# Attention and bilinear kernel: k's stack apart, each load behind its buffer's last use, four weighing visits, and a first unit on VectorE with more filler matmuls

## The chip, the core and the metric

The kernel runs on one core of one Trainium2 chip. The metric is the device time of one execution in microseconds (us). TensorE (PE) multiplies matrices; its weight loads are listed apart as PEld. VectorE is DVE, ScalarE is ACT, GpSimd is POOL, and SyncE (SP) issues the DMAs. TensorE writes to PSUM, which has eight banks; everything else lives in SBUF.

## The reference

```python
q_rot, k_rot = rotate(q), rotate(k)              # 4 batches, 8 heads, 576 positions, 64 wide
attn = softmax(q_rot @ k_rot.T / 8)
x = (attn @ v)                                   # as 2304 tokens x 512
h = elu(x @ w_in) @ w_out                        # 512 -> 2048 -> 512
out = ((h @ w1) * (h @ w2)) @ w3 @ w_out2        # 512 -> 1024 -> 512
```

All in float32. `rotate` multiplies by tables of cosines and sines and adds the two halves.

## The kernel before

The attention is a list of 16 **units** (a batch and a pair of heads). A unit has nine **steps**: four chunks of 128 queries times two heads, and one step for the last 64 queries of both heads. In step n of the loop at line 496 TensorE makes the scores `s` of the step two ahead (L286; L278 for the last step of a unit and for the whole first unit), then what the table `todo` holds for step n, then the four transposes `ptp` of the probabilities of step n (L334). VectorE takes the row maximum (`nm`, L298), ScalarE the exponential (`pr`, L302). The transposes are copied out of PSUM in the next step by ScalarE or VectorE (L316, L318). All this is written in a fixed order per engine (`manual_schedule`), and each engine works its list in order.

The values are weighed in **visits**: `weigh` multiplies the transposed probabilities with v into a PSUM tile `o` (L392, 64-column products, two halves of a unit's queries; L394 and L397 for the last 64 keys, tile `plT`), and one step after the last visit of a half VectorE multiplies by the reciprocal sums into `xT` (L406). Six visits of L392 and two of L394 fall on a unit.

The next unit's q and k are rotated meanwhile: on POOL two products (`turn`, L184), a sum (`add`, L187), then ScalarE copies the high part of the float32r split (`high`, L80), and POOL subtracts for the low part (`low`, L193). `stack` then moves the parts by DMA into tile `st` (L260, L263), from which the scores read. POOL also spreads the reciprocals (`rb`, L84), fills `diag` (L84), and does the last step of one weight tile in each of twelve units (L125), each time in the first step of units 2 to 13. ROPE and STACK give the steps of these pieces, NORM, SPREAD, NTURN and PV those of the weighing.

The first unit is rotated in pieces before the loop (`first_rope`), shared by VectorE and POOL. `warm_up` issues matmuls of a tile of zeros, which write nothing that is used. After the attention come the two feed-forward parts, whose text is the same in both kernels.

Of the kernel before, what the change touches and what calls it, by code (L numbers as in the profile page):

```python
# [18 lines left out]
P = 128  # L19
# [38 lines left out]
def kernel(  # L58
# [81 lines left out]
    with ExitStack() as c1:  # L140
# [94 lines left out]
        def first_rope(u):  # L235
            for w, at_, to, eng, steps in (
                (1, 0, 352, dve, (0, 1, 2)), (0, 0, 256, dve, (0, 1, 2)),
                (1, 0, 352, dve, (3, 4)), (0, 0, 256, dve, (3, 4)),
                (1, KD, SK, pool, (0, 1, 2)), (1, 352, KD, dve, (0, 1, 2)), (1, 352, SK, dve, (3, 4)),
                (0, 256, S, pool, (0, 1, 2)),  # L240
            ):
# [9 lines left out]

        def stack(u):

            st = stacks[u] = st_p.tile([P, 2, 3, S], F32R, tag="st", name="st")
            for j in range(2):
                c = (SK, S)[j]
                for e in range(2):
                    part = hls[u][64 * j:64 * j + 64, e].bitcast(F32)
                    both = part[:, :2 * c].rearrange("p (w c) -> p w c", w=2)[:, :, :S]
                    nc.sync.dma_start(st[64 * e:64 * e + 64, j, 0:2].bitcast(F32), both)  # L260
                for e in range(2):
                    part = hls[u][64 * j:64 * j + 64, 1 - e].bitcast(F32)
                    nc.sync.dma_start(st[64 * e:64 * e + 64, j, 2].bitcast(F32), part[:, c:c + S])  # L263

# [56 lines left out]
        def turn(g):  # L321
# [60 lines left out]

        def weigh(n, u, hf, kc):
            nq = HALF[hf][1]
            if kc == 0:
# [4 lines left out]
            if kc < 4:  # L390
                for j in range(2):
                    pe.matmul(o[64 * j:64 * j + 64], vj[:, j, kc], th[:, j, kc], start=(kc == 0), stop=False)  # L392
                return
            pe.matmul(o[:, :256], vs[u][:, 2 * NKC * D:], tl[:, :256], start=False, stop=not hf)  # L394
            if hf:
                for j in range(2):
                    pe.matmul(  # L397
                        o[64 * j:64 * j + 64, 256:], vj[:64, j, 4], tl[:64, 256 + 64 * j:320 + 64 * j],
                        start=False, stop=True,
                    )  # L400
            at(n + 1, weighed, u, hf)

# [29 lines left out]
        for i, u in enumerate(units):  # L432
            n = 9 * i
            if i + 2 < len(units):
                at(n + LOAD_QK, load, units[i + 2], 1)
                at(n + LOAD_QK, load, units[i + 2], 0)
            if i + 1 < len(units):
                v_ = units[i + 1]
                at(n + LOAD_V, load_v, v_)
                if i == 0:  # L440
                    steps = part(u, 0, 256, S, dve, act, dve)
                    for k_ in (3, 4):
                        at(FIRST[0][k_ - 3], steps[k_])
                    at(FIRST[0][2], diagonal, u)
# [34 lines left out]
        with tc.manual_schedule():  # L479
# [277 lines left out]
```

## Time and profile before

| | |
|---|---|
| device time, median of 3 runs | 1051.91 us (1050.37 to 1052.35) |
| the profiled execution | 1052.59 us, span 1050.8 us |
| TensorE busy | 1037.8 us, 99% of the span |
| POOL busy between 40 and 250 us | 0.82 to 0.90 of the time |
| granted TensorE clock, mean | 0.986 |

The span is what the trace covers; the profiled execution's own time is 1.8 us longer. A busy TensorE is not one at its peak: ends of matmuls are modelled. The attention takes the first 305 us, the rest is matmuls of 512 columns.

### The profile page before, as it was taken

The page shows a single profiled execution, that of the slowest core. Times are in us where ns is not written, and L with a number is a line of the kernel's source. Part 1 is how long each engine was busy: PE and PEld are TensorE (multiplying, and loading weights), DVE is VectorE, ACT ScalarE, POOL GpSimd, SP SyncE. Part 2 cuts the span into 40 slices and gives each one's busy share as a digit, 9 for nine tenths or more (in the row PEclk, how much of TensorE's full clock was granted, in tenths as well). Part 3 has the DMA queues.
Part 4 walks back from the last instruction along what each step waited for, and adds up shares of the span by engine and source line. Part 5 has one row for each costly group of instructions (what it writes and reads, how often), then busy time and mean ns, then how long its engine had stood idle before and what let it go on. Part 6 is the DMA issues. An engine that isn't in the chain of part 4 may idle for free.

```text
span 1050.8 us, 14641 instructions
## 1 busy us (share of the span) xinstructions
PE 1037.8 (99%) x5590; PEld 865.4 (82%) x5590; DVE 568.3 (54%) x978; ACT 463.7 (44%) x921; POOL 257.9 (25%) x260
## 2 busy tenths in 40 slices
PE   8999999999999999999999999999999999999998
PEld 7767767777777888888888999989888888889997
DVE  4678878778767996668667653212313214122321
ACT  2567666667546756556545644322211212112121
POOL 4698889888510010001000000000100000000000
PEclk7799999999999999999999999999999999999999
DMA  4687878786756015545555523536400101001000
GB/s 157 190 233 213 232 221 216 211 236 198 172 211 242 1 40 180 180 160 180 181 180 180 181 101 127 193 120 220 143 0 1 41 1 41 1 1 41 1 31 31
DMA packets 46390, 138.84 MB, mean 132 GB/s; under 512 B 5488, under 2 KB 7152, under 8 KB 46320
## 3 DMA queue, kind: packets, MB, share of 16 engines
q1 hardware_dynamic: 46320, 137.91, 41.6%
q8 instruction: 44, 0.72, 0.3%
q14 instruction: 26, 0.21, 0.1%
HBM read 85.66 MB, written 25.69 MB: 106 GB/s over the span
## 4 chain that ended last, share of the span: by engine, by line
PE 90%; SPq 3%; DMA 3%; DVE 1%; POOL 1%; issue 1%; ACTq 0%; ACT 0%; DVEq 0%
PE h L537 19%; PE y L564 19%; PE a L537 9%; PE b L537 9%; PE y L674 9%; PE ptp L334 6%; PE o L392 5%; PE s L286 5%; PE w L615 4%; DMA st<-hl 3%; PE s L278 2%; SPq L263 2%; SPq L260 1%; PE o L394 1%; POOL hl L193 1%
## 5 line engine op out<-in xcount | busy, mean ns | idle before, releaser
L537 PE MATMUL h<-xt,w 128*128 128x512 f32 (+1 forms) x960 | 213.4, 368 | 0.0
L564 PE MATMUL y<-g,w 128*128 128x512 f32 (+1 forms) x960 | 212.5, 367 | 0.0
L537 PEld LDWEIGHTS h<-xt,w 128*128 128x128 f32 x960 | 175.2, 188 | 23.4 <-DVE e L552 0.2
L564 PEld LDWEIGHTS y<-g,w 128*128 128x128 f32 x960 | 175.2, 188 | 22.5
L76 POOL TENSOR_TENSOR xt<-xT,xt 128x512 fp32r<-128x512 f32 (+1 forms) x20 | 26.5, 1326 | 668.9 <-DVE xt L82 668.1
L302 ACT ACTIVATE pr<-s,nm 128x576 f32<-128x576 f32 x144 | 107.0, 743 | 100.8 <-DVE nm L298 99.9
L661 DVE TENSOR_TENSOR a<-b,a 128x512 f32<-128x512 f32 (+1 forms) x40 | 25.5, 637 | 180.0 <-PE b L537 180.0
L298 DVE TENSOR_REDUCE nm<-s 128x1 f32<-128x576 f32 x144 | 108.6, 754 | 25.7 <-PE s L286 11.7
L537 PE MATMUL a<-xt,w 128*128 128x512 f32 (+1 forms) x480 | 107.4, 368 | 0.0
L537 PE MATMUL b<-xt,w 128*128 128x512 f32 (+1 forms) x480 | 106.8, 367 | 0.0
L674 PE MATMUL y<-W,g 128*128 128x512 f32 x432 | 104.9, 390 | 0.0
L334 PEld LDWEIGHTS ptp<-idt,pr 128*128 128x128 f32 x576 | 63.4, 144 | 46.2 <-issue 23.7
L286 PE MATMUL s<-st 128*128 128x288 f32 x480 | 94.9, 316 | 4.4 <-DMA st<-hl 4.3
L537 PEld LDWEIGHTS a<-xt,w 128*128 128x128 f32 x480 | 88.2, 188 | 12.5
L537 PEld LDWEIGHTS b<-xt,w 128*128 128x128 f32 x480 | 87.7, 188 | 11.3
L334 PE MATMUL ptp<-idt,pr 128*128 128x128 f32 x576 | 96.4, 291 | 0.0
L674 PEld LDWEIGHTS y<-W,g 128*128 128x128 f32 x432 | 80.9, 188 | 16.1
L659 ACT ACTIVATE a<-a 128x512 f32<-128x512 f32 (+1 forms) x40 | 22.3, 556 | 139.2 <-PE a L537 139.2
L552 DVE SCALAR_TENSOR_TENSOR e<-e,h 128x512 f32<-128x512 f32 (+1 forms) x80 | 50.3, 631 | 61.1 <-ACT e L550 60.7
L184 POOL TENSOR_TENSOR raw_qk<-raw_qk,tab 128x640 f32<-128x640 f32 (+1 forms) x56 | 82.5, 1483 | 2.3
L549 ACT ACTIVATE e<-h 128x512 f32<-128x512 f32 (+1 forms) x80 | 44.2, 554 | 72.6 <-PE h L537 70.2
L286 PEld LDWEIGHTS s<-st 128*128 128x128 f32 x480 | 67.9, 189 | 7.0 <-issue 3.8
(301 smaller groups left out, 1275.0 us busy)
## 6 DMA issues: line engine op xcount, KB each, us to landing
kept<-w SPq DMA_DIRECT2D x40, 512.0 KB, 2.6
w<-kept SPq DMA_DIRECT2D x40, 512.0 KB, 3.3
st<-hl SPq DMA_DIRECT2D x60, 288.0 KB, 4.5
raw<-w_ SPq DMA_DIRECT2D x32, 512.0 KB, 3.6
raw_qk<-k_ SPq DMA_DIRECT2D x15, 640.0 KB, 6.1
raw_qk<-q_ SPq DMA_DIRECT2D x15, 576.0 KB, 5.1
st<-hl SPq DMA_DIRECT2D x60, 144.0 KB, 4.2
raw<-w_in_ SPq DMA_DIRECT2D x16, 512.0 KB, 5.1
```

The lines of the kernel that those rows point to most:

```text
L184: pool.tensor_tensor(r[:, z], r[:, z], tab[:, w, z, TAB[w]], op=ALU.mult)
L286: pe.matmul(s[:, n, :288], st[:, j, 0, c * P:c * P + P], st[:, j, z, n * 288:(n + 1) * 288], start=(z == 1), stop=(z == 2),)
L298: dve.tensor_reduce(nm, s[:, :, :288], axis=AX.XY, op=ALU.max, negate=True)
L302: act.activation(pr_t[u, c][:, j].rearrange("p (n i) -> p n i", n=2), s[:, :, :288], ACTF.Exp, bias=nm, accum_out=sums_t[u, hf][:, at_:at_ ...
L334: pe.transpose(pt[:, kc], pr[:, at_:at_ + P], idt)
L392: pe.matmul(o[64 * j:64 * j + 64], vj[:, j, kc], th[:, j, kc], start=(kc == 0), stop=False)
L537: pe.matmul(ps[:, :n], w[:, a, cc * P:(cc + 1) * P], x[cc][:, c], start=(i == 0), stop=(i == 11))
L549: act.activation(e, ps[:, :n], ACTF.Relu, scale=-1.0)
L552: dve.scalar_tensor_tensor(g, e, -1.0, ps[:, :n], op0=ALU.add, op1=ALU.max)
L564: pe.matmul(ys[ti][o][:, :n], wout[f][:, a, o * P:(o + 1) * P], g[:, c], start=(f == 0 and i == 0), stop=(f == NF - 1 and i == 2),)
L615: pe.matmul(ps, w3_t[i, j // 4][:, a, j % 4 * P:j % 4 * P + P], wo[j][:, c], start=(j == 0 and n == 0), stop=(j == 7 and n == 2),)
L674: pe.matmul(outs[ti][o], g[:, a, o * P:(o + 1) * P], wW[f][:, c], start=(f == 0 and i == 0), stop=(f == NG - 1 and i == 2),)
```

## The change

1. `stack(u, w)` runs for k and q apart, each right behind its own `low`; twelve DMAs of 144 KB take the place of four of 288 and four of 144 KB. q's `low` moves from step 4 to 3, k's from step 2 to -2.
2. A load of q or k is issued behind the `low` that frees its buffer, instead of both at step 4.
3. `weigh` takes several key chunks at once: four visits in place of six, with the L394 and L397 products inside them (the 64-key product now over 128 rows, below zeros).
4. PSUM: `ps_o` has one bank instead of two, `ps_t` three instead of two.
5. The first unit's rotation is on VectorE alone; POOL starts with the second unit's k. 30 filler matmuls at the start instead of 27, 4 more inside the first score, and 34 in the first eleven steps instead of 8.

```diff
-NTURN = (5, 11)
+NTURN = (6, 11)
 PV = (
-    (5, 0, (0,)), (6, 0, (1,)), (7, 0, (2, 3)), (8, 0, (4,)),
-    (10, 1, (0,)), (11, 1, (1,)), (12, 1, (2, 3)), (13, 1, (4,)),
+    (5, 0, (0, 1)), (7, 0, (4, 2, 3)), (10, 1, (0, 1)), (12, 1, (4, 2, 3)),
 )
-ROPE = ((-1, 0, 1, 1, 4), (-5, -4, -3, -3, 2))
-STACK = 4
+ROPE = ((-1, 0, 1, 1, 3), (-5, -4, -3, -3, -2))
+DIAG = 5
-WARM = 27
-FILL = (4, 2, 2)
+WARM = 30
+FILL = (4, 3, 4, 4, 4, 3, 3, 3, 2, 2, 2)
+FILL_IN = 4
...
-        ps_o = c1.enter_context(tc.tile_pool(name="ps_o", bufs=2, space=PSUM, reuse_waits="tile"))
-        ps_t = c1.enter_context(tc.tile_pool(name="ps_t", bufs=2, space=PSUM, reuse_waits="tile"))
+        ps_o = c1.enter_context(tc.tile_pool(name="ps_o", bufs=1, space=PSUM, reuse_waits="tile"))
+        ps_t = c1.enter_context(tc.tile_pool(name="ps_t", bufs=3, space=PSUM, reuse_waits="tile"))
...
             def low():
                 pool.tensor_tensor(lo, r[:, 0], hi.bitcast(F32), op=ALU.subtract)
-                if w == 0:
-                    diagonal(u)
+                stack(u, w)
+                m = units.index(u) + 2 - w
+                if m < len(units):
+                    load(units[m], 1 - w)
...
-                (1, KD, SK, pool, (0, 1, 2)), (1, 352, KD, dve, (0, 1, 2)), (1, 352, SK, dve, (3, 4)),
-                (0, 256, S, pool, (0, 1, 2)),
+                (1, 0, 352, dve, (3, 4)), (0, 0, 256, dve, (3, 4)), (1, 352, SK, dve, (0, 1, 2, 3, 4)),
```

Where POOL's list changes: one unit's worth in the middle of the attention. `raw_qk` 640 wide is k, 576 wide is q. Before:

```order
L84 TENSOR_SCALAR rb<-ri 128x256
L193 TENSOR_TENSOR hl<-raw_qk,hl 128x576
L84 TENSOR_SCALAR diag_108<-hl 64x2x64 x2
L184 TENSOR_TENSOR raw_qk<-raw_qk,tab 128x640 x2
L187 TENSOR_TENSOR raw_qk<-raw_qk 128x640
L184 TENSOR_TENSOR raw_qk<-raw_qk,tab 128x576
L125 TENSOR_TENSOR w<-wr,w 128x512
L84 TENSOR_SCALAR rb_113<-ri 128x256
L84 TENSOR_SCALAR rb_113<-ri 64x64 x2
...
L187 TENSOR_TENSOR raw_qk<-raw_qk 128x576
L193 TENSOR_TENSOR hl<-raw_qk,hl 128x640
```

And the same unit after the change:

```order
L83 TENSOR_SCALAR rb<-ri 128x256
...
L83 TENSOR_SCALAR diag_108<-hl 64x2x64 x2
L184 TENSOR_TENSOR raw_qk<-raw_qk,tab 128x640
L187 TENSOR_TENSOR raw_qk<-raw_qk 128x640
L193 TENSOR_TENSOR hl<-raw_qk,hl 128x640
L184 TENSOR_TENSOR raw_qk<-raw_qk,tab 128x576
L124 TENSOR_TENSOR w<-wr,w 128x512
L83 TENSOR_SCALAR rb_114<-ri 128x256
L83 TENSOR_SCALAR rb_114<-ri 64x64 x2
...
L187 TENSOR_TENSOR raw_qk<-raw_qk 128x576
L193 TENSOR_TENSOR hl<-raw_qk,hl 128x576
```

(A second L184 of the same size is left out of the lists where it would only repeat.) Each `low` (L193) now stands directly behind its `add` (L187); before, other work of POOL stood between them.

Where TensorE's list changes: steps 5 to 7 of the third unit. Before, with `ptr` the transposed reciprocals:

```order
L375 MATMUL ptr_826<-idt_58,rb_112 128x128 x2
L392 MATMUL o_831<-ptT_693,v__620 64x256 x2
L334 MATMUL ptp_836<-idt_58,pr_730 128x128 x4
L278 MATMUL s_842<-hl_339,diag0_108 128x288 x6
...
L334 MATMUL ptp_859<-idt_58,pr_785 128x128 x4
L286 MATMUL s_865<-st_797 128x288 x4
```

After:

```order
L288 MATMUL s_869<-st_456 128x288 x4
L404 MATMUL o_879<-ptT_754,v__666 64x256 x4
L336 MATMUL ptp_885<-idt_58,pr_793 128x128 x4
L280 MATMUL s_891<-hl_363,diag0_108 128x288 x6
L377 MATMUL ptr_904<-idt_58,rb_113 128x128 x2
L336 MATMUL ptp_911<-idt_58,pr_855 128x128 x4
L288 MATMUL s_917<-st_700 128x288 x4
L394 MATMUL o_879<-plT_755,v__666 128x256
```

The visits of steps 5 and 6 have become one in step 5, and step 6 has only the transposed reciprocals beside its score. (Before, a second L392 stood between L278 and L334.)

Where VectorE's list changes: the first unit, from the pieces of k above column 352 on. Before:

```order
L215 TENSOR_TENSOR raw_qk<-raw_qk,tab 128x68 x2
L219 TENSOR_TENSOR raw_qk<-raw_qk 128x68
L229 TENSOR_TENSOR hl<-raw_qk,hl 128x288
L298 TENSOR_REDUCE nm<-s 128x1 x3
L215 TENSOR_TENSOR raw_qk<-raw_qk,tab 128x576 x2
L298 TENSOR_REDUCE nm<-s 128x1
L231 SCALAR_TENSOR_TENSOR hl<-raw_qk,hl 128x320
```

After:

```order
L218 TENSOR_TENSOR raw_qk<-raw_qk,tab 128x288 x2
L222 TENSOR_TENSOR raw_qk<-raw_qk 128x288
L232 TENSOR_TENSOR hl<-raw_qk,hl 128x288
L300 TENSOR_REDUCE nm<-s 128x1 x3
L218 TENSOR_TENSOR raw_qk<-raw_qk,tab 128x320 x2
L222 TENSOR_TENSOR raw_qk<-raw_qk 128x320
L218 TENSOR_TENSOR raw_qk<-raw_qk,tab 128x576 x2
L300 TENSOR_REDUCE nm<-s 128x1
L234 SCALAR_TENSOR_TENSOR hl<-raw_qk,hl 128x320
```

Between the third and the fourth `nm` VectorE now has the first unit's q above column 256 as well; POOL had it before.

## Rows read from the trace of the kernel before

**Rows 1.** Timeline of PE: four of the sixteen L278 groups with `diag`, one a unit.

```profile
55.24 1.03 PE L278 MATMUL s<-hl,diag 128*128 128x288 f32 x6
...
161.79 1.03 PE L278 MATMUL s<-hl,diag 128*128 128x288 f32 x6
...
178.89 1.03 PE L278 MATMUL s<-hl,diag 128*128 128x288 f32 x6
...
302.26 1.03 PE L278 MATMUL s<-hl,diag 128*128 128x288 f32 x6
```

**Rows 2.** Timeline inside one unit: start, us, engine, operation [idle before <-releaser].

```profile
161.43 0.48 DVE L406 TENSOR_TENSOR xT<-o,R 128x320 f32<-128x320 f32 x1
...
162.75 0.20 PEld L392 LDWEIGHTS o<-ptT,v__1785 128*64 128x64 f32 x4 [0.17 <-issue]
...
163.33 0.42 PEld L334 LDWEIGHTS ptp<-idt,pr 128*128 128x128 f32 x4 [0.39 <-issue]
...
164.44 0.63 PEld L392 LDWEIGHTS o<-ptT,v__1785 128*64 128x64 f32 x8 [0.16 <-issue]
...
165.45 0.42 PEld L334 LDWEIGHTS ptp<-idt,pr 128*128 128x128 f32 x4 [0.39 <-ACT hl L80]
...
166.06 0.57 PEld L286 LDWEIGHTS s<-st 128*128 128x128 f32 x4
...
166.89 0.76 DVE L298 TENSOR_REDUCE nm<-s 128x1 f32<-128x576 f32 x1
...
167.56 0.57 PEld L286 LDWEIGHTS s<-st 128*128 128x128 f32 x4
...
167.69 0.74 ACT L302 ACTIVATE pr<-s,nm 128x576 f32<-128x576 f32 x1 [0.94 <-DVE nm L298]
...
168.59 0.57 PEld L286 LDWEIGHTS s<-st 128*128 128x128 f32 x4
```

**Rows 3.** Waits of PE over the span: total us, times, longest.

```profile
PE s L286 <- DMA st<-hl: 4.3, 10, 0.9
```

**Rows 4.** Windows, one unit: PE, PEld, DVE, ACT, POOL busy, PEclk, DMA share, GB/s.

```profile
161.85:178.96 17.11, 17.11 (x128) 12.62 (x126) 14.34 (x27) 12.21 (x29) 15.59 (x15) 1.00 0.76 209
```

**Rows 5.** Timeline of POOL in that unit: the two rows with idle time.

```profile
166.44 0.93 POOL L84 TENSOR_SCALAR rb<-ri 128x256 f32<-128x256 f32 x3 [0.41 <-PE ptl__2052 L342]
...
172.45 0.49 POOL L84 TENSOR_SCALAR rb<-ri 128x256 f32<-128x256 f32 x1 [0.56 <-DVE ri L358]
```

**Rows 6.** Windows at the start: columns as in Rows 4.

```profile
11.00:12.00 1.00, 0.00 (x0) 0.00 (x0) 0.97 (x2) 0.00 (x0) 0.95 (x2) 0.97 0.00 0
13.00:39.00 26.00, 26.00 (x103) 20.89 (x102) 13.10 (x21) 9.37 (x22) 13.53 (x15) 0.50 0.44 119
...
39.00:40.00 1.00, 1.00 (x8) 0.58 (x8) 0.76 (x1) 0.09 (x1) 1.00 (x2) 0.87 1.02 221
```

**Rows 7.** Timeline of the first unit, all engines.

```profile
9.74 1.48 DVE L215 TENSOR_TENSOR raw_qk<-raw_qk,tab 128x68 f32<-128x68 f32 x2
...
14.38 1.49 DVE L298 TENSOR_REDUCE nm<-s 128x1 f32<-128x576 f32 x2 [1.17 <-PE s L278]
...
19.53 1.42 DVE L215 TENSOR_TENSOR raw_qk<-raw_qk,tab 128x576 f32<-128x576 f32 x2
...
24.01 0.73 ACT L80 ACTIVATE hl<-raw_qk 128x640 fp32r<-128x640 f32 x1
...
24.82 1.54 POOL L229 TENSOR_TENSOR hl<-raw_qk,hl 128x640 fp32r<-128x640 f32 x1 [7.08 <-ACT hl L80]
...
31.13 3.06 SPq L260 DMA_DIRECT2D st<-hl  x2
...
37.12 2.70 SPq L263 DMA_DIRECT2D st<-hl  x2
...
40.07 0.76 PE L286 MATMUL s<-st 128*128 128x288 f32 x4
```

**Rows 8.** Tile `st` from 40 to 300 us: its DMAs.

```profile
DMA to landing us min/median/max: 3.1/4.4/6.6
```

More of the change, by code (lines that the diff above doesn't have):

```diff
@@ L36 @@
 LOAD_QK = 4
-ROPE = ((-1, 0, 1, 1, 4), (-5, -4, -3, -3, 2))
-STACK = 4
+ROPE = ((-1, 0, 1, 1, 3), (-5, -4, -3, -3, -2))
+DIAG = 5
 FIRST = ((0, 1, 4), (0, 0, 0, 1, 2), (0, 0, 3, 3, 4), 2)
-KD = 420
-WARM = 27
-FILL = (4, 2, 2)
+WARM = 30
+FILL = (4, 3, 4, 4, 4, 3, 3, 3, 2, 2, 2)
+FILL_IN = 4
 EVAC_ACT = (1, 0, 0, 1, 0, 0, 0, 0, 1, 0, 1, 0)
@@ L158 @@
         two = cst.tile([P, D], F32, name="two")
+        pl1 = cst.tile([P, 384], F32, name="plT1")
         zero = cst.tile([P, 1, 1], F32, name="zero")
@@ L237, in first_rope @@
                 (1, 0, 352, dve, (0, 1, 2)), (0, 0, 256, dve, (0, 1, 2)),
-                (1, 0, 352, dve, (3, 4)), (0, 0, 256, dve, (3, 4)),
-                (1, KD, SK, pool, (0, 1, 2)), (1, 352, KD, dve, (0, 1, 2)), (1, 352, SK, dve, (3, 4)),
-                (0, 256, S, pool, (0, 1, 2)),
+                (1, 0, 352, dve, (3, 4)), (0, 0, 256, dve, (3, 4)), (1, 352, SK, dve, (0, 1, 2, 3, 4)),
             ):
@@ L250, in diagonal, with stack @@
                 copy_hi(diag[units.index(u) % 2][h, :, h], hls[u][h, :, 512:S].bitcast(F32), pool)
-        def stack(u):
-            st = stacks[u] = st_p.tile([P, 2, 3, S], F32R, tag="st", name="st")
+        def stack(u, w):
+            if u not in stacks:
+                stacks[u] = st_p.tile([P, 2, 3, S], F32R, tag="st", name="st")
+            st = stacks[u]
             for j in range(2):
[L256 to L263, printed above, removed]
+                c = (0, (SK, S)[j])[w]
+                for z in ((0,), (1, 2))[w]:
+                    for e in range(2):
+                        part = hls[u][64 * j:64 * j + 64, (e, 1 - e)[z == 2]].bitcast(F32)
+                        nc.sync.dma_start(st[64 * e:64 * e + 64, j, z].bitcast(F32), part[:, c:c + S])
         HALF = ((0, 256), (256, 320))
@@ L275, in scores @@
                 at_ = S + 64 * (c == 4 or j == 0)
-                for i, (a, e) in enumerate(PAIRS):
-                    for n in range(2):
+                for n in range(2):
+                    if n and g == seq[0]:
+                        warm_up(FILL_IN)
+                    for i, (a, e) in enumerate(PAIRS):
                         pe.matmul(
@@ L327, in turn @@
                     pt_p.tile([P, 2, 4, nq], F32, tag=f"pt{hf}", name="ptT"),
-                    pt_p.tile([P, nq + 64 * hf], F32, tag=f"pl{hf}", name="plT"),
+                    pl1 if hf else pt_p.tile([P, nq], F32, tag="pl0", name="plT"),
                 ]
@@ L381, with weigh @@
         o_t = {}
-        def weigh(n, u, hf, kc):
+        def weigh(n, u, hf, kcs):
             nq = HALF[hf][1]
-            if kc == 0:
+            if kcs[0] == 0:
                 o_t[u, hf] = ps_o.tile([P, nq], F32, tag="o", name="o", padded_shape=[P, 512])
@@ L389, in weigh @@
             vj = vs[u][:, :2 * NKC * D].rearrange("p (j k d) -> p j k d", j=2, k=NKC)
-            if kc < 4:
-                for j in range(2):
[L392 to L401, printed above, removed]
+            for kc in kcs:
+                if kc == 4:
+                    pe.matmul(o[:, :256], vs[u][:, 2 * NKC * D:], tl[:, :256], start=False, stop=False)
+                    if hf:
+                        for j in range(2):
+                            pe.matmul(
+                                o[64 * j:64 * j + 64, 256:], vj[:, j, 4], tl[:, 256 + 64 * j:320 + 64 * j],
+                                start=False, stop=False,
+                            )
+                    continue
+                for j in range(2):
+                    pe.matmul(o[64 * j:64 * j + 64], vj[:, j, kc], th[:, j, kc], start=(kc == 0), stop=(kc == 3))
+            if kcs[-1] == 3:
+                at(n + 1, weighed, u, hf)
         def weighed(u, hf):
@@ L433 @@
             n = 9 * i
-            if i + 2 < len(units):
-                at(n + LOAD_QK, load, units[i + 2], 1)
-                at(n + LOAD_QK, load, units[i + 2], 0)
+            if i == 0:
+                at(LOAD_QK, load, units[2], 1)
+                at(LOAD_QK, load, units[2], 0)
+                at(LOAD_QK + 1, load, units[3], 1)
             if i + 1 < len(units):
@@ L441 @@
                     steps = part(u, 0, 256, S, dve, act, dve)
-                    for k_ in (3, 4):
-                        at(FIRST[0][k_ - 3], steps[k_])
+                    for k_ in range(5):
+                        at(FIRST[0][max(k_ - 3, 0)], steps[k_])
                     at(FIRST[0][2], diagonal, u)
@@ L449 @@
                     at(FIRST[2][4], diagonal, v_)
-                    at(FIRST[2][4], stack, v_)
+                    at(FIRST[1][4], stack, v_, 1)
+                    at(FIRST[2][4], stack, v_, 0)
                 else:
@@ L455 @@
                             at(n + d, lambda v_=v_, w=w, k_=k_: steps_of[v_, w][k_]())
-                    at(n + STACK, stack, v_)
+                    at(n + DIAG, diagonal, v_)
             for hf in range(2):
@@ L461 @@
             for t, hf, kcs in PV:
-                for kc in kcs:
-                    at(n + t, weigh, n + t, u, hf, kc)
+                at(n + t, weigh, n + t, u, hf, kcs)
         at(4, lambda: pool.tensor_tensor(two, idt[:, :D], idt[:, D:], op=ALU.add))
@@ L491 @@
             pool.memset(rb[1][:, 2], 0.0)
+            pool.memset(pl1[64:, 256:], 0.0)
             for g in seq[:AHEAD]:
```

## The prediction

> **What bounds the kernel now.** I read the timeline of TensorE first. One score group with `diag` falls on each unit, so their distance is a unit's period: the fastest is 178.89 - 161.79 = 17.10 us, and from the second unit (55.24) to the last (302.26) fourteen periods take 247.02, 17.64 each [rows 1]. Inside the fast unit I then looked for gaps of TensorE. The reader is to see that there are none but one kind: where a visit to `o` (64-column weights) begins, the weight load idles 0.16 to 0.17 us, and 0.39 before the transposes behind it [rows 2]. So 17.10 is TensorE's own floor, and 14 x 0.54 = 7.6 us are waits. The list of waits names one, on the DMA into `st`, 4.3 us in 10 cases [rows 3]; the rest of the 7.6 is not named. POOL is close behind: in the fast unit its instructions are busy 15.59 of 17.11 us [rows 4], and only 0.41 + 0.56 = 0.97 us are idle with a name, both on the reciprocals [rows 5]; its loop without waits is thus 17.11 - 0.97 = 16.14. Last, the clock at the start: TensorE had nothing to do when the granted clock fell between 11 and 12 us, and it came back between 39 and 40 [rows 6]. The unit in between ran at half speed. The feed-forward parts are unchanged and begin when the attention lets go of TensorE, so what the attention loses or gains is the answer.
>
> **The four visits.** A visit with 4 products costs 0.17 + (163.33 - 162.75) = 0.75 us, one with 8 costs 0.16 + (165.45 - 164.44) = 1.17 [rows 2]. Four products are 0.42, so 0.33 is the price of the visit. Six become four: 0.66 less per unit. The `plT` products ride along; I take their cost as before, since they need the same switch either way. TensorE's floor would go from 17.10 to 16.44.
>
> Two things are given back. First, only one bank holds `o`, so a visit waits until `xT` of the half before is done. The `xT` of step 4 now stands in a step that is a score and transposes alone, as short as 168.59 - 167.56 = 1.03 us. The visit of step 5 could start about 1.03 + 0.5 + 0.16 = 1.7 after step 4's score. `xT` stands behind that score's `nm`, which starts 0.83 after the score (166.06 to 166.89) and ends at about 1.6, and takes 0.48: done at 2.1 [rows 2]. Wait: 0.4. Second, a score needs the exponential of two steps before to be over; that takes 167.69 + 0.74 - 166.06 = 2.37 from the start of that score [rows 2]. Steps 8 and 0 are both short now (about 1.15 and 1.03), together 2.2: wait 0.2. TensorE's floor after the change: 16.44 + 0.4 + 0.2 = 17.0. If both waits hide behind work that I have not seen, it is 16.4; if each doubles, 17.6.
>
> **k's stack apart.** The same bytes move, and behind q's `low` only four DMAs are left of eight. Between q's `low` in step 3 and the first score from it in step 7 lie four steps, some 8 us, against issue and a landing of 4.4 us in the median, 6.6 at most [rows 8]; so the wait for `st` goes away as such. But POOL's list puts each `low` directly behind its `add`. ScalarE must copy the high part in between, and POOL can do nothing else meanwhile. In the first unit this copy took 0.73, and POOL began 0.08 after it (24.01 + 0.73 = 24.74, then 24.82) [rows 7]; so a hole of 0.73 + 0.08 = 0.8 twice per unit. Before, other instructions of POOL stood there. POOL's loop: 16.14 + 2 x 0.8 = 17.7 us in the twelve units with a weight tile, more than TensorE's 17.0. POOL can't run ahead, since k's copy stands in ScalarE's list behind an exponential of step 6. From there to q's `low` is a little over half of its loop, about 10 us, and the copy and the landing of 4.4 use up what is left before the next step 7. So I let POOL set twelve periods and TensorE two: 12 x 17.7 + 2 x 17.0 = 246.4, less some 0.4 that the first one has in hand: 246.0 against 247.0. **Gain 1.0.** From below: were POOL no bound, 14 x 16.44 = 230, and with the waits 14 x 17.0 = 238. From above: ScalarE may be in an exponential when `add` ends; if every hole is longer by that 0.74 x half, the loop is 18.4 and the sum 12 x 18.4 + 34 = 255.
>
> **Loads by their buffers** cost nothing: they are issued at least half a period ahead of their first use, and this slack hides them. In the first unit alone they stand in SP's list between k's and q's stack (below).
>
> **The first unit.** Three more matmuls at the start, six instructions at about 0.11, end the fillers near 9.9 us. VectorE alone turns k's last 288 columns in three instructions of some 0.45 (576 columns take 0.71 with POOL idle [rows 7]), and with the copy its low part ends near 11.2, where TensorE has been kept busy by the four inner fillers until 11.0. The first score is then whole at 11.5, while before its maximum began at 14.38 [rows 7]. If the clock stays up, a step of the first unit is fillers 0.85, score 0.76, transposes 0.4, about 2.0 us, and TensorE reaches step 7 near 30. There it needs the second unit's `st`. VectorE, with `nm` and the rotation in one list, finishes q's low part near 26.3. SP then still has to get rid of eight DMAs of k's stack from POOL's `low` (ends near 22) and two loads; the eight DMAs of before were issued from 31.13 to 37.12 + 2.70 = 39.8, 8.7 us for 1.73 MB [rows 7], so k's 1.15 MB take 5.8 and q's stack is issued from 28.5, its first half lands near 33.5. Before this score was at 40.07 [rows 7]: 6.6 earlier. From there to the next `diag` took 55.24 - 40.07 = 15.2. After, four steps carry two fillers each (4 x 0.43 = 1.7), and ScalarE meets a copy whose `add` is late, because k's load of the third unit stood behind k's stack (0.7): 17.6, so `diag` at 51.1. **Gain 4.2.** If the filling hides nothing and `st` is 2 us later, 2; if `st` is in time at 30, 7.
>
> **The tail.** The last unit gives up two visits: 0.7.
>
> Sum: 1.0 + 4.2 + 0.7 = 5.9 on the profiled execution's 1052.59, thus 1046.7. That execution is 0.7 above the median of the three runs, so I give 1046.0. Bounds of this case: 1041 to 1050.
>
> **Rivals.** *The clock falls all the same.* The score of step 2 waits for q's low part above column 256, which stands behind a `nm` and five rotations in VectorE's list. The third `nm` ends near 14.6 (first score 11.5, maximum and exponential that free its bank 1.5, third score 0.8, its maximum 0.8). Adding 0.45, 0.45, 0.48, 0.71, 0.71, `nm` 0.7 and 0.48 gives 18.6, while TensorE is there at 17: it idles 1.5 us but for two matmuls. Before, it was idle for all of the slice in which the clock fell [rows 6]. POOL works on the second unit's k until about 15.4, and beside POOL two products of 68 columns took 1.48, as long as two of 576 with POOL idle [rows 7]; that makes the gap 2.3. The Trainium skill, "SBUF — State Buffer", section "Who interferes with whom", says that a VectorE instruction with two inputs in SBUF contends with a GpSimd instruction that reads SBUF, and that the pair of ports is an exclusive lock; the trace agrees with its 1.48. By that rule the sum above stays as it is while the clock holds, since the wait for `st` in step 7 hides the 0.8; but this rival would be the likelier one. For it speaks also that TensorE was busy all the time from 13 to 39 us and stayed at 0.50 [rows 6]. Against it: here the gap has matmuls in it. Price: steps 3 to 6 double, some 2 us each, less what `st` hides: `diag` at 56.8, 1.6 later than before; with the other two terms 1052.59 - 0.1, thus 1051.8. Chance 0.28.
>
> *POOL is no bound*, because ScalarE's copy starts at once and small gaps in POOL's list close. Then TensorE's 17.0 holds: 238 against 247, gain 9, with the rest 14: 1038. For it: 0.55 of the 16.14 are gaps between instructions. Against: nothing can stand in the holes. Chance 0.17.
>
> *Slower: the holes are longer.* ScalarE works in order; with an exponential ahead of the copy the hole is 0.8 + 0.4, POOL's loop 18.4, the fourteen periods 255: 8 lost, 4.9 won back: 1055. It decides from a loop of 18.05 on (12 x 0.4 = 4.9). For it: ScalarE is busy 12.21 of 17.11 us [rows 4]. Against: where POOL is late, ScalarE already waits at the copy. Chance 0.12.
>
> My forecast has the remaining 0.43. Changes under 0.2% (2.1 us) can't be told from none. Faster: all but a tenth of 0.43, all of 0.17, and 0.07 of the 0.28, in which the first score's lead survives: 0.63. Same: 0.04 + 0.17 = 0.21. Slower: 0.12 and 0.04 of the fallen clock: 0.16. The range goes from 1036, past the third case, to 1055: what is left out is the slower case's upper half and mixtures, under 0.2.
>
> **What would show it.** In the profile after: a granted clock of 1.00 from 5 to 50 us (step one), `diag` of the second unit near 51; periods near 17.7 with POOL busy 0.9 and its `low` waiting on ScalarE's copy about 0.8 us, twice a unit; weight loads for `o` idle before four visits, and waits of `o` on `xT`; none on `st` after the second unit. Wrong it is if periods fall below 17.2 or rise above 18.1, or the clock is 0.50 for long.

## The result, and the profile after

The change made the kernel slower: 1058.53 us median of 4 runs (1057.8 to 1060.19) against 1051.14 (1049.77 to 1052.35), ratio 1.0075 [1.0049, 1.0100]. The forecast was 1046.0, faster. The profiled execution took 1059.03, its span is 1057.2.

Timeline of PE in the changed kernel, the same four `diag` groups as in [rows 1] by their place in the program (second, eighth, ninth and last unit):

```profile
57.84 1.03 PE L280 MATMUL s<-hl,diag 128*128 128x288 f32 x6
...
167.15 1.03 PE L280 MATMUL s<-hl,diag 128*128 128x288 f32 x6
...
185.36 1.03 PE L280 MATMUL s<-hl,diag 128*128 128x288 f32 x6
...
309.29 1.04 PE L280 MATMUL s<-hl,diag 128*128 128x288 f32 x6
```

The reader is to see two losses. The second `diag` comes at 57.84 instead of 55.24: 2.6 lost, where 4.2 were forecast as won. From there to the last one it takes 251.45 instead of 247.02: 4.4 lost, where 1.0 was forecast as won. Together 7.0, and the tail gives 0.6 back (from the last `diag` to the end of the span 747.9 instead of 748.5). That is the 6.4 by which the spans differ.

Windows of the changed kernel, columns as in [rows 4]: two stretches of the start, a unit with a weight tile, one of the last three without.

```profile
33.00:36.00 3.00, 0.00 (x0) 0.00 (x0) 0.00 (x0) 0.53 (x3) 2.92 (x4) 1.00 1.05 255
36.00:43.00 7.00, 4.94 (x20) 3.19 (x20) 1.25 (x3) 1.57 (x3) 5.65 (x7) 0.51 1.01 276
167.15:185.36 18.21, 16.52 (x129) 12.78 (x127) 14.62 (x26) 12.20 (x29) 15.63 (x16) 1.00 0.76 217
275.22:292.25 17.03, 16.50 (x128) 12.76 (x127) 11.81 (x23) 11.07 (x27) 11.51 (x13) 1.00 0.59 145
```

**The start.** TensorE kept its clock of 1.00 to 33 us, as forecast, and then stood still for 5 us with all 16 DMA engines busy; after that the granted clock was 0.51. What it waited for, on SP and PE:

```profile
21.34 5.96 SPq L263 DMA_DIRECT2D st<-hl  x8
27.39 0.53 SPq L167 DMA_DIRECT2D raw_qk<-k_  x1
27.97 0.59 SPq L167 DMA_DIRECT2D raw_qk<-q_  x1
28.66 2.79 SPq L263 DMA_DIRECT2D st<-hl  x4
...
38.06 1.30 PE L288 MATMUL s<-st 128*128 128x288 f32 x4 [5.20 <-DMA st<-hl]
```

q's stack was issued at 28.66 (forecast 28.5), but the first score from it began only at 38.06: ahead of it were k's stack and the two loads, 640 and 576 KB, that stand between the stacks. From issue to landing the four DMAs of q's stack took 8.5 us and more (first line); in experiment 14 (below), where no load stands between the stacks, all twelve of k's and q's took 2.3 to 2.7 (second line):

```profile
DMA to landing us min/median/max: 8.5/8.7/8.8
DMA to landing us min/median/max: 2.3/2.5/2.7
```

In the profiles of experiments 1, 2, 3, 5, 6, 9 and 13, which have the same order on SP in the first unit, this score comes at 37.83 to 38.93. In that of 12 it comes at 35.88 without a wait; why its stack landed in time stays open.

**The periods.** Eleven periods are 18.2, the last three 17.03 (the forecast and the expectations reckoned with twelve; the first of the twelve weight tiles falls ahead of the second `diag`). Inside an 18.2 unit, first POOL (compare [rows 5]):

```profile
131.53 1.56 POOL L187 TENSOR_TENSOR raw_qk<-raw_qk 128x640 f32<-128x640 f32 x1
134.40 1.55 POOL L193 TENSOR_TENSOR hl<-raw_qk,hl 128x640 fp32r<-128x640 f32 x1 [1.31 <-DMA v__1610<-v_]
...
141.03 1.41 POOL L187 TENSOR_TENSOR raw_qk<-raw_qk 128x576 f32<-128x576 f32 x1
143.24 1.41 POOL L193 TENSOR_TENSOR hl<-raw_qk,hl 128x576 fp32r<-128x576 f32 x1 [0.79 <-ACT hl L79]
144.62 0.84 POOL L83 TENSOR_SCALAR rb<-ri 128x256 f32<-128x256 f32 x1
145.43 1.96 POOL L184 TENSOR_TENSOR raw_qk<-raw_qk,tab 128x640 f32<-128x640 f32 x1
```

The holes before the two `low` are there: 0.79 for q, as forecast, but 1.31 for k. The DMA named there has long landed; it was ScalarE's copy:

```profile
132.59 0.74 ACT L304 ACTIVATE pr<-s,nm 128x576 f32<-128x576 f32 x1 [1.27 <-DVE nm L300]
...
133.32 0.38 ACT L381 ACTIVATE R<-ptr 128x256 f32<-128x256 f32 x1
133.58 0.73 ACT L79 ACTIVATE hl<-raw_qk 128x640 fp32r<-128x640 f32 x1
```

k's `add` ended at 133.09, but the copy began only at 133.58, behind an exponential that itself waited for its maximum. Why TensorE's side is late shows on VectorE and PEld in steps 2 to 5:

```profile
141.35 1.12 DVE L359 TENSOR_SCALAR ri<-sums 128x4 f32<-128x4 f32 x1
...
144.17 1.02 DVE L112 SCALAR_TENSOR_TENSOR wr<-raw,wr 128x512 int32<-128x512 int32 x1
145.23 0.77 DVE L115 SCALAR_TENSOR_TENSOR wr<-raw,wr 128x512 int32<-128x512 int32 x1
145.92 0.41 DVE L320 COPY plT<-ptl__1785 128x256 f32<-128x256 f32 x1
146.26 0.74 DVE L300 TENSOR_REDUCE nm<-s 128x1 f32<-128x576 f32 x1
146.92 0.48 DVE L411 TENSOR_TENSOR xT<-o,R 128x320 f32<-128x320 f32 x1
...
147.47 0.66 PEld L404 LDWEIGHTS o<-ptT,v__1610 128*64 128x64 f32 x8 [1.69 <-issue]
```

VectorE has no gap from 140.69 to `xT`. Its L359, of 128x4 elements, lasts 1.12 and ends at 142.47, 0.03 after POOL's `add` (141.03 + 1.41). Then come the steps of the weight tile, and the visit waits 1.69 for `xT`, 0.16 of which a visit has without any wait [rows 2]. I had priced that wait at 0.4.

### The profile page after: what moved, and what is told of

It reads as the page before. It is cut to its first block, busy times and chain, and to the rows that moved or that the text cites. A ratio compares the mean times of both kernels' runs of the same rounds, so it can differ in the third digit from the quotient of the medians.

```text
span 1057.2 us, 14855 instructions
## 1 busy us (share of the span) xinstructions
PE 1023.1 (97%) x5656; PEld 866.6 (82%) x5656; DVE 573.6 (54%) x981; ACT 462.1 (44%) x921; POOL 253.9 (24%) x255
## 4 chain that ended last, share of the span: by engine, by line
PE 94%; issue 2%; DVE 2%; ACT 1%; DMA 1%; SPq 0%; ACTq 0%
PE h L544 19%; PE y L571 19%; PE a L544 9%; PE b L544 9%; PE y L681 9%; PE o L404 7%; PE s L288 6%; PE ptp L336 6%; PE w L622 4%; PE s L280 2%; PE o L394 1%; DVE nm L300 1%; PE warm L481 1%; ACT pr L304 1%; DMA st<-hl 1%
## 5 line engine op out<-in xcount | busy, mean ns | idle before, releaser
L300 DVE TENSOR_REDUCE nm<-s 128x1 f32<-128x576 f32 x144 | 108.0, 751 | 23.4 <-PE s L288 15.8
L336 PE MATMUL ptp<-idt,pr 128*128 128x128 f32 x576 | 90.7, 280 | 0.0
L184 POOL TENSOR_TENSOR raw_qk<-raw_qk,tab 128x640 f32<-128x640 f32 (+1 forms) x56 | 87.6, 1564 | 5.6 <-issue 3.4
L336 PEld LDWEIGHTS ptp<-idt,pr 128*128 128x128 f32 x576 | 65.4, 143 | 28.5 <-issue 9.2
```

The costliest lines, as they stand in the source:

```text
L300: dve.tensor_reduce(nm, s[:, :, :288], axis=AX.XY, op=ALU.max, negate=True)
L336: pe.transpose(pt[:, kc], pr[:, at_:at_ + P], idt)
```

## The experiments

"Second `diag`" and "period" are of the profiled execution; the ratio is to runs of the kernel before on the same chip.

| kernel | second `diag` | period in units with a weight tile | median us | ratio |
|---|---|---|---|---|
| changed | 57.84 | 18.21 | 1058.53 | 1.0075 [1.0049, 1.0100] |
| 1 two banks | 56.77 | 18.22 | 1059.92 | 1.0077 [1.0051, 1.0103] |
| 2 lows later | 58.12 | 18.4 to 20.2 | 1067.21 | 1.0148 [1.0110, 1.0187] |
| 3 POOL copies | 58.03 | 18.56 | 1062.49 | 1.0099 [1.0063, 1.0134] |
| 4 loads around | 53.44 | 18.21 | 1053.89 | 1.0017 [0.9997, 1.0037] |
| 5 weights later | 56.32 | 17.28 | 1047.85 | 0.9962 [0.9945, 0.9978] |
| 6 lows and weights | 57.46 | 23.4 to 26.9 | 1138.39 | 1.0825 [1.0795, 1.0855] |
| 7 visits alone | 50.37 | 17.14 to 18.98 | 1050.99 | 0.9989 [0.9973, 1.0004] |
| 8 lows, weights, start | 48.79 | 23.3 to 26.5 | 1136.68 | 1.0813 [1.0779, 1.0846] |
| 9 xT first | 57.79 | 18.22 | 1056.94 | 1.0053 [1.0041, 1.0066] |
| 10 weights, start | 49.85 | 17.28 | 1040.02 | 0.9894 [0.9882, 0.9907] |
| 11 weights, before | 54.07 | 18.3 to 20.6 | 1072.68 | 1.0194 [1.0169, 1.0219] |
| 12 one weight step | 52.79 | 17.57 | 1050.76 | 0.9998 [0.9984, 1.0012] |
| 13 extra maximum | 57.26 | 19.8 to 21.6 | 1091.23 | 1.0372 [1.0355, 1.0389] |
| 14 start alone | 49.36 | 18.22 | 1050.24 | 0.9986 [0.9973, 1.0000] |

The profiled executions of 7 and 12 took 1047.71 and 1047.16, some 3.5 under their medians: their start was faster than in most of their runs, and so their second `diag` is early.

### Which wall sets the period: 1 to 3

```diff
-tile_pool(name="ps_o", bufs=1, ...), tile_pool(name="ps_t", bufs=3, ...)
+tile_pool(name="ps_o", bufs=2, ...), tile_pool(name="ps_t", bufs=2, ...)
```

> The changed kernel with the PSUM banks of before: two for `o`, two for the transposes; all else stays. In the changed kernel twelve periods are 18.21 us and TensorE idles 1.5 us in each before the visit of step 5. Theory A (POOL's list and ScalarE's are one ring: `add` of POOL, copy on ScalarE, `low` of POOL, with ScalarE's copy of k standing behind an exponential that comes late): with a second bank the visit and so the exponential come earlier, k's copy can start at the end of `add` instead of 0.49 after it, and periods fall to 18.21 - 0.49 = 17.7; 12 x 0.5 = 6 us, 1058.5 - 6 = 1052.5. Theory B (the one bank of `o` alone sets the period): the 1.5 us go, TensorE's own 17.0 remains, 1058.5 - 12 x 1.2 = 1044. Theory C (POOL's holes alone, the bank has no part): 18.2 and 1058.5.

Nothing moved. TensorE no longer waits for `o`, but for the bank of `plT`, which VectorE copies out of the same list, 1.1 us ahead of `xT`:

```profile
108.87 0.42 PEld L336 LDWEIGHTS ptp<-idt,pr 128*128 128x128 f32 x4 [1.39 <-DVE plT L320]
```

So B, in which the bank alone is to blame, has fallen, and A's 17.7 too; VectorE's list was not cleared by this.

```diff
-ROPE = ((-1, 0, 1, 1, 3), (-5, -4, -3, -3, -2))
+ROPE = ((-1, 0, 1, 1, 4), (-5, -4, -3, -3, 2))
```

> The changed kernel with q's `low` back in step 4 and k's in step 2 of the unit, as before, so that other work of POOL stands between each `add` and its `low`; the stack is still apart for k and q, with one bank for `o`. Theories A and C (the holes of 1.31 and 0.80 us between `add` and `low` close the ring): both holes go, POOL's loop is 18.2 - 2.1 = 16.1, and TensorE's 17.0 sets the period: 1058.5 - 12 x 1.2 = 1044. Theory B (the bank of `o`): the wait of 1.5 us before the visit of step 5 stays, periods stay at 18.2 and the time at 1058.5. Second rival: k's stack, issued 4 steps later, lets scores wait for `st`: 17.3 to 17.8, 1048 to 1054.

The holes are gone and it got slower, so A and C fell as the whole cause. POOL now has time to wait, and TensorE waits as long as before for `o`, because L115 takes 1.94:

```profile
163.56 0.41 POOL L83 TENSOR_SCALAR rb<-ri 128x256 f32<-128x256 f32 x1 [1.95 <-DVE ri L360]
...
165.93 1.94 DVE L115 SCALAR_TENSOR_TENSOR wr<-raw,wr 128x512 int32<-128x512 int32 x1
...
169.33 0.66 PEld L404 LDWEIGHTS o<-ptT,v__1846 128*64 128x64 f32 x8 [1.89 <-issue]
```

```diff
             def high():
-                copy_hi(hi, r[:, 0], act)
+                copy_hi(hi, r[:, 0], pool)
```

> The changed kernel with the high parts of the units from the third on copied by POOL instead of ScalarE, so that POOL never waits for a copy. POOL took 1.26 us for a copy with scaling of 128x1280, thus an estimate of 0.63 for k's 128x640 and 0.57 for q's 128x576, against holes of 1.31 and 0.80. Theories A and C: the ring shortens by (1.31 - 0.63) + (0.80 - 0.57) = 0.9, periods 17.3, time 1058.5 - 12 x 0.9 = 1047.7, and ScalarE's exponentials no longer stand behind a copy. Theory B (the bank of `o`): no change, 18.2, 1058.5.

Slower, 18.56: TensorE waits 1.57 to 1.78 for `o` as before. And POOL still waits, now for TensorE:

```profile
133.46 0.73 POOL L83 TENSOR_SCALAR hl<-raw_qk 128x640 fp32r<-128x640 f32 x1 [0.69 <-PE s L280]
```

Its copy of k overwrites a buffer of `hl` (there are two) from which the diagonal score of the unit two before still reads (here until 133.30), and it waits like this twelve times (0.69 to 0.72). So this edit did not cut POOL loose from TensorE: it took ScalarE out of the ring and left the ring closed. After these three I took it for two walls of nearly one height (theory D).

### The start: 4

```diff
-                at(LOAD_QK, load, units[2], 1)
-                at(LOAD_QK, load, units[2], 0)
+                at(FIRST[1][4], load, units[2], 1)
+                at(LOAD_QK + 1, load, units[2], 0)
```

> The changed kernel with the loads of the third unit moved in SP's list: k's ahead of the second unit's stack of k, q's behind its stack of q; nothing stands between the two stacks. In the changed kernel TensorE stands still from 32.9 to 38.1 us for the second unit's `st`, the granted clock then is 0.50 until about 42.6, and the second `diag` comes at 57.84. Theory (the loads between the stacks make `st` late, and the stop costs the clock): the 1.22 MB of loads no longer pass ahead of q's stack, the first score from `st` comes near 32, the clock stays at 1.00, the second `diag` falls near 50, and the time near 1058.5 - 8 = 1050.5, with the later periods unchanged at 18.2. Rival (the DMA engines have too much to move in any order): the score stays near 38, the time at 1058.5. Second rival (what is won at the start is lost because the third unit's q comes late): second `diag` near 50, third unchanged at 76, the time at 1058.5.

The wait for `st` is gone (first score from it at 35.82, no idle time), and 4.6 us are won. 3.4 of the forecast gain are missing. In this profile the clock fell earlier, at the gap where the first unit's q is late (my first rival's place):

```profile
20.41 0.79 PE L280 MATMUL s<-hl 64*128 64x288 f32 x4 [1.07 <-DVE hl L234]
```

```profile
20.00:27.00 7.00, 6.59 (x32) 5.93 (x33) 5.39 (x9) 3.50 (x8) 3.68 (x5) 0.64 0.70 203
```

In the changed kernel the gap was 1.05 at the same place and the clock stayed at 1.00. The runs of 4 agree with the clock as the reason: the three with a mean granted clock of 0.999 or more took 1051.15 to 1052.55, the other seven (0.995 to 0.997) 1053.09 to 1056.65.

### VectorE's list: 5, 6 and 8

```diff
-PF, PF_AT, PF_STEP, STEPS, DLEAD = 6, 10, 9, (0, 1, 2, 2, 3, 8), 6
+PF, PF_AT, PF_STEP, STEPS, DLEAD = 6, 10, 9, (0, 1, 4, 6, 7, 8), 6
```

> The changed kernel with VectorE's two long weight steps (L112, L115) moved from step 3 to steps 5 and 7 of a unit, ScalarE's last one with them; POOL's list and the PSUM banks stay. Theory D (two walls of nearly one height: POOL's ring with its holes gives 18.2, and VectorE's crowded list in steps 2 to 4, which makes `xT` late and TensorE wait 1.5 us for the bank of `o`, gives 18.4): the wait at the visit of step 5 shrinks from 1.5 to some 0.3, k's copy comes earlier by what its exponential does, and POOL's ring alone remains, 18.2 - 0.49 = 17.7: 1058.5 - 12 x 0.5 = 1052.5; bound from the other side, if ScalarE keeps the copy late, 18.2 and 1058.5. Theory B (the one bank with VectorE's list is the only wall): 17.0 to 17.2 and 1045.

(STEPS are the steps of a weight tile's six pieces, counted from step 1 of a unit; the third and fourth are L112 and L115, the fifth ScalarE's copy.) Two instructions of VectorE and the copy in other steps win 10.7 us, 9.7 of them in the fourteen periods of the profile (241.71 instead of 251.45): 17.28, less than D's 17.7, more than B's 17.0 to 17.2. Three rows of POOL:

```profile
112.71 1.57 POOL L193 TENSOR_TENSOR hl<-raw_qk,hl 128x640 fp32r<-128x640 f32 x1 [0.85 <-DMA raw<-w_in_]
...
121.55 1.42 POOL L193 TENSOR_TENSOR hl<-raw_qk,hl 128x576 fp32r<-128x576 f32 x1 [0.80 <-ACT hl L79]
122.93 0.41 POOL L83 TENSOR_SCALAR rb<-ri 128x256 f32<-128x256 f32 x1
...
125.57 1.94 POOL L184 TENSOR_TENSOR raw_qk<-raw_qk,tab 128x640 f32<-128x640 f32 x1
```

k's hole is 0.85 and `rb` 0.41 instead of 0.84; one L184 is still 1.94, now beside L112.

Experiment 6 has the edits of 2 and 5, experiment 8 those of 2, 4 and 5 and the FIRST of experiment 10.

> Both at once: `low` of q and k back in steps 4 and 2 (no holes in POOL's list) and VectorE's two long weight steps moved to steps 5 and 7. Each wall of theory D is taken down; the one with the lows alone gave 18.4 and more. Theory D: neither wall stands, TensorE's own 17.0 to 17.3 sets the periods, 12 x 1.0 less than the changed kernel: 1058.5 - 12 = 1046 (the start is unchanged). Rival (a third wall, such as `st` issued late behind k's `low` of step 2, which let some periods of the lows-later kernel go to 19 and 20): periods of 17.5 to 18.5 and waits on the DMA into `st`, 1050 to 1062.

> The kernel with both walls taken down (lows in steps 4 and 2, long weight steps in steps 5 and 7), the loads of the third unit around the second unit's stacks, and in the first unit VectorE's low part of the first q ahead of the third maximum and of the second unit's q, so that TensorE does not stand still near 20 us, where the kernel with only the loads moved lost its clock to 0.64 in the stretch from 20 to 27. Theory: the clock stays at 1.00 from 5 us on, the second `diag` comes near 49, then periods of 17.0 to 17.3: 1058.5 - 8.5 - 12 = 1038. Rival (the walls come back, as in the kernel with the lows alone): second `diag` near 49 and periods of 18.2, 1050. Second rival (the clock falls all the same): second `diag` near 53, 1042.

Both failed by far, and for a reason that no theory had. The waits of 6:

```profile
POOL w L124 <- ACT w L120: 53.5, 10, 6.4
...
PE s L288 <- DMA st<-hl: 49.6, 9, 7.2
```

POOL's L124 stands ahead of the lows in its list and now waits for ScalarE's copy of step 8; so the lows, the stacks behind them and the scores that read them come late. In 5 k's `low` is done before L124. Of 8 the first unit counts: clock 1.00 throughout and the second `diag` at 48.79, as expected.

### Parts on the kernel before: 7 and 11

Experiment 7 puts PV, NTURN and `weigh` of the change into the kernel before, with the banks of before; 11 puts the STEPS of experiment 5 there.

> The kernel before with the four visits alone (and the row of transposed reciprocals in step 6); lows, stacks, loads, two banks for `o` and two for the transposes as before. If a visit saves 0.33 us as the rows of before say, TensorE's floor falls from 17.10 by 0.66 and is given back up to 0.2 by two short steps: fast periods 16.6, the fourteen 14 x 0.5 = 7 us shorter: 1052.5 - 7 = 1045.5, if POOL (16.1) and VectorE let it. Theory D (VectorE's crowded list is near its wall as soon as visits end a step earlier): the transposes wait for their bank instead, periods 17.3 to 17.7, 1048 to 1053. Rival (the visits themselves cost time): slower than before, over 1054.

> The kernel before with one edit: VectorE's two long weight steps in steps 5 and 7. It tells whether their place hurt the kernel before as well. Theory (in the kernel before `xT` has a second bank and a step more, so the place costs nothing there): the fourteen periods stay near 247, time within 2 us of 1051.5. Rival (the place costs both kernels alike): fourteen periods of 17.1, 240, and 1044. Second rival (POOL, whose last weight step waits for ScalarE's copy, then stands in front of the lows, as in the kernel with lows and weight steps moved): periods over 20, above 1080.

The visits alone are worth nothing that can be told (the interval holds 1). A fast period has TensorE busy 16.86 instead of 17.11 [rows 4], and the transposes behind the visit wait instead:

```profile
162.79 0.42 PEld L334 LDWEIGHTS ptp<-idt,pr 128*128 128x128 f32 x4 [0.53 <-DVE plT L318]
```

In 11 POOL's last weight step waits for ScalarE's copy, 36.8 us in 12 cases: the mechanism of 6, with a smaller price than the expectation's. So the place of the weight steps that helps the changed kernel harms the one before.

### What the ring is made of: 9, 12 and 13

```diff
-                at(n + 1, weighed, u, hf)
+                at(n + 1, weighed, u, hf, first=bool(hf))
```

> The changed kernel with one edit: in step 4 VectorE does the product into `xT` of the second half ahead of that step's row maximum instead of behind it; POOL's and ScalarE's lists, the weight steps and the banks stay. The runs so far say that two banks (18.2), no holes in POOL's list (18.4) and copies on POOL (18.6) each leave the period, while moving VectorE's two long weight steps brings it to 17.28. Theory E (the ring of the changed kernel runs from POOL's sum of q through VectorE's list to `xT`, from there through the bank of `o` to the diagonal score, its exponential, k's copy and back to POOL): `xT` comes some 0.6 us earlier (one maximum of 0.74 less ahead of it, the wait for a later one not in the way), periods 17.6, 1058.5 - 12 x 0.6 = 1051.3. Rival F (what the weight steps cost is their meeting with POOL's instructions, which they lengthen from 1.55 to 1.96 and from 0.41 to 0.84, and not what stands behind them on VectorE): these meetings stay, 18.2, 1058.5.

The period stayed at 18.22. The wait for `o` went, and the transposes of step 4 wait up to 1.5 us for the copy of `plT`; E, which ran through `xT`, fell in that form.

```diff
-PF, PF_AT, PF_STEP, STEPS, DLEAD = 6, 10, 9, (0, 1, 2, 2, 3, 8), 6
+PF, PF_AT, PF_STEP, STEPS, DLEAD = 6, 10, 9, (0, 1, 2, 6, 7, 8), 6
```

> The changed kernel with only the second of VectorE's two long weight steps (L115) moved, from step 3 to step 7 of a unit; L112 stays in step 3. What is open is how the 0.93 us that moving both gave per period divides. Mixed theory (the period of 18.21 is POOL's own loop of 17.72, of which 0.43 is `rb` lengthened beside L112 and 0.41 an L184 lengthened beside L115, and 0.49 more in which k's copy comes late because VectorE's crowded list frees TensorE's PSUM banks late): the L184 is 1.55 again, `rb` stays at 0.84, and VectorE's list is 0.77 shorter, which is more than 0.49, so k's hole is 0.8: 17.3. Theory E (only VectorE's list counts): 18.21 - 0.77 = 17.44. Theory F (only the lengthened instructions of POOL count): 18.21 - 0.41 = 17.80. In time: 1058.5 - 12 x 0.9 = 1047.6, 1049.3 or 1053.6.

17.57: not E's 17.44, not F's 17.80, and 0.26 over the mixed theory. POOL:

```profile
119.53 0.84 POOL L83 TENSOR_SCALAR rb<-ri 128x256 f32<-128x256 f32 x1
120.34 1.54 POOL L184 TENSOR_TENSOR raw_qk<-raw_qk,tab 128x640 f32<-128x640 f32 x1
...
126.77 1.65 POOL L193 TENSOR_TENSOR hl<-raw_qk,hl 128x640 fp32r<-128x640 f32 x1 [0.98 <-DMA raw<-w_out_]
```

The lengthened `rb` and the restored L184 are as that theory says; k's hole is 0.98, not 0.80, and its `low` 0.10 longer. What is not lengthened in POOL's round, without holes, is 18.21 - 1.31 - 0.79 - (0.84 - 0.41) - (1.96 - 1.55) = 15.27. With the holes and lengthenings of 12 that gives 15.27 + 0.80 + 0.98 + 0.43 + 0.10 = 17.58 (measured 17.57), with those of 5 15.27 + 0.80 + 0.85 + 0.39 = 17.31 (17.28). This is bookkeeping, since the holes and lengthenings are read from each kernel: it shows that POOL has no other idle time in these periods, not what sets k's hole at 1.31, 0.98 and 0.85. The 0.10 has a reason on VectorE: L115, now in step 7, ran until 127.01, and this `low` began at 126.77:

```profile
126.36 0.65 DVE L115 SCALAR_TENSOR_TENSOR wr<-raw,wr 128x512 int32<-128x512 int32 x1
```

```diff
             dve.tensor_reduce(nm, s[:, :, :288], ...)
+            if (c, j) == (2, 1):
+                more = sm_p.tile([P, 1], F32, tag="more", name="more")
+                dve.tensor_reduce(more, s[:, :, :288], ...)
```

> The changed kernel with one more row maximum (0.75 us, out of PSUM, its result unused) on VectorE in step 3 of each unit, behind that step's own; nothing else is touched. Mixed theory and theory E (VectorE's list in step 3 stands in the ring): periods of 18.21 + 0.75 = 18.96 in the twelve units with a weight tile, 1058.5 + 12 x 0.75 = 1067.5, and k's hole on POOL grows from 1.31 to 2.06. Theory F (POOL's list with its lengthened instructions alone): 18.2 and 1058.5.

F fell: 0.75 us more on VectorE alone cost 1.6 to 3.3 us a period. More than the 0.75, because the list, moved by it, meets POOL elsewhere (L115 takes 1.93 instead of 0.77), TensorE waits 2.33, and the clock falls in mid-attention:

```profile
115.00:120.00 5.00, 2.67 (x13) 1.40 (x13) 4.04 (x6) 2.49 (x6) 4.76 (x5) 0.73 0.97 307
120.00:125.00 5.00, 5.00 (x24) 4.64 (x25) 2.60 (x4) 1.73 (x4) 0.17 (x2) 0.59 0.22 86
```

### Both losses mended: 14 and 10

Experiment 14 is 4 with q's low part of the first unit ahead of the third maximum (and the products of the second unit's q a step later); experiment 10 is 14 with the weight steps of 5.

```diff
-FIRST = ((0, 1, 4), (0, 0, 0, 1, 2), (0, 0, 3, 3, 4), 2)
+FIRST = ((0, 0, 4), (0, 0, 0, 1, 2), (1, 1, 3, 3, 4), 2)
```

> The changed kernel with the two edits of the first unit alone: the third unit's loads around the second unit's stacks, and q's low part ahead of the third maximum. The weight steps stay in step 3. Theory (the late second `diag` and the long periods are two separate losses): clock 1.00 throughout, second `diag` near 49.5 instead of 57.84, later periods unchanged at 18.2 in twelve and 17.0 in the rest: 1058.5 - 8.3 = 1050.2. Rival (the ring of POOL takes the lead back, because with an earlier start POOL is the later one from the third unit on): second `diag` near 49.5, third no earlier than 73, 1055.

> The changed kernel with three edits: VectorE's two long weight steps in steps 5 and 7, the third unit's loads around the second unit's stacks, and q's low part of the first unit ahead of the third maximum. The first alone gave 1047.85 and periods of 17.28, with the second `diag` at 56.32; the two others, beside lows that were later, brought the second `diag` to 48.79 with a clock of 1.00. Theory (start and periods add up): 1047.85 - (56.3 - 48.8) = 1040.3. Rival (the clock falls in the first unit as in the kernel with only the loads moved): second `diag` near 53, 1044.5. Second rival (an earlier start is paid back by late loads of the third unit): third `diag` near 73 as with the weight steps alone, 1047.

Both came out as expected: 1050.24 and 1040.02. In 14 the first score from `st` comes without a wait and the second `diag` 16.5 behind it:

```profile
32.88 0.77 PE L288 MATMUL s<-st 128*128 128x288 f32 x4
...
49.36 1.03 PE L280 MATMUL s<-hl,diag 128*128 128x288 f32 x6
```

The two losses are separate and add up: 8.3 for the start, and 10.2 more for the weight steps. Windows of 10:

```profile
13.00:33.00 20.00, 19.05 (x139) 16.04 (x137) 15.69 (x25) 9.19 (x21) 13.39 (x14) 1.00 0.61 158
33.00:43.00 10.00, 10.00 (x81) 8.24 (x80) 5.76 (x13) 7.16 (x16) 6.89 (x8) 1.00 0.96 294
```

Experiment 10 beats the changed kernel by 18.5 us and the one before by 11.

## Why the prediction was wrong

**The first unit (forecast 4.2 won, 2.6 lost).** The step that failed is "q's stack is issued from 28.5, its first half lands near 33.5". The issue was right to 0.2; the landing is 4.6 late. The sum gave the two loads in between no more than time to issue (28.5 - 22 - 5.8 = 0.7), and nothing for the 1.22 MB that they put ahead of q's stack: it reckoned 5.0 from issue to landing, and it took 8.5 to 8.8. The stop cost twice, since the clock fell in it: from the first score to the `diag` took 19.8, forecast 17.6. 4.6 and 2.2 are the 6.7 by which the second `diag` missed its 51.1. Experiments 14 and 10, without the stop, have this score at 32.9 and 33.4, as forecast, and the `diag` 16.5 later, at 49.4 and 49.9; so the 17.6 was itself 1.1 too long, and the clock cost 3.3. The rival of the fallen clock had another place, the gap near 20 us. There the clock held in the changed kernel's profile and in those of 3, 6 and 9, and fell in those of 1, 2, 4, 5, 12 and 13, which have the same pieces of q there: in six of ten profiles, against a chance of 0.28. That it held in this profile is luck, as far as is known.

**The wait for the one bank (0.4).** Mis-sized: 1.5 to 1.7. I took it from a stretch of VectorE in which no weight step stands [rows 2]. In the units with a weight tile three of them and a lengthened L359 stand ahead of `xT`. In the last three, without, the period is 17.03 and TensorE's forecast of 17.0 holds: this visit's weight load idles 0.53 (row below), 0.37 more than the usual 0.16, and in experiment 9, which does `xT` ahead of the maximum, the last two periods are 16.65 and 16.63, 0.4 less. TensorE is busy 16.50 instead of 17.11, the 0.6 of the forecast; but in experiment 7, with the same visits and two banks, it is 16.86, so the 0.6 are not shown to be the visits' alone.

```profile
290.79 0.66 PEld L404 LDWEIGHTS o<-ptT,v__3485 128*64 128x64 f32 x8 [0.53 <-PE s L288]
```

**POOL's loop (17.7).** Its size without the extra 0.52 of k's hole is 18.21 - 0.52 = 17.69, as forecast, and by the forecast's parts: without its holes the round is 18.21 - 1.31 - 0.79 = 16.11, against 16.14. Of this, 0.84 is instructions lengthened beside VectorE. The unit read in the kernel before held about as much (0.76): `rb` 0.49 instead of 0.41, and `diag`, 0.67 after the change, took

```profile
174.40 1.35 POOL L84 TENSOR_SCALAR diag<-hl 64x128 fp32r<-64x128 f32 x2
```

As the period the 17.7 failed. The step that failed is the size of k's hole, 0.8 where the runs show 1.31, because POOL's round closes over TensorE: POOL's `add` of q holds up VectorE, VectorE's crowded list frees TensorE's banks late, the diagonal score and its exponential come late, and k's copy stands behind them. That VectorE's list is a link is shown by 5, 12 and 13; the order of the links in between is read from the rows. Eleven times 0.52 are 5.7 us, against an error of 5.4 in the fourteen periods. My slower rival named this copy behind an exponential, with a decision from 18.05 on, and had 0.12; it held for one of its two holes.

**What held.** No wait for `st` after the second unit; the hole of q, 0.8; the tail, 0.6. "Wrong if periods rise above 18.1" came true.

That L359 waits for POOL's `add`, and L115 for POOL's L184, is read from their ends, not tried alone. The Trainium skill, "SBUF — State Buffer", section "Who interferes with whom", says that the two engines' shared ports are an exclusive lock: who is second stands still for the other's whole instruction. The rows agree in both directions: 0.16 became 1.12 on VectorE, 0.41 became 0.84 on POOL. Why the transposes of step 4 got another bank in 9 stays open.

## What to carry to other kernels

Price a new wait in the most crowded unit, not in the one that is easiest to read: list all that stands ahead of the releasing instruction on its engine, and what runs on the engine with which it shares ports. An issue time is not a landing time: count the bytes issued ahead. When two engines' lists close a ring, undoing one link only moves the wait to the next resource that the same list frees; look for what the links have in common.

## What was not expected of the hardware

An instruction of VectorE on 128x4 elements lasted 1.12 us instead of 0.16, and L109 in experiment 5 1.61 instead of 0.40, each while POOL was in an `add`. The granted clock also fell in the middle of the attention, to a mean of 0.59 in 5 us, after a wait of TensorE of 2.33 us; at the start a gap of 1.05 left it at 1.00 in one kernel's profile and one of 1.07 did not in another's. The other profiles with this first unit agree: gaps of 0.72 to 0.98 left it (3, 6, 9), one of 1.37 did not (2, 5, 12, 13), nor a stop of 1.89 just ahead of the place (1).
